# An RWKV-5 and top-1 routing kernel: which engine makes one unit's product of r and k, when the next one's starts, and how many filling products stand between

## The chip, the cores and the metric

The kernel runs on one core of a Trainium2 chip. Its engines work from queues of their own: TensorE (PE, with its weight loads as PEld), VectorE (DVE), ScalarE (ACT), GpSimd (POOL) and SyncE (SP), which issues most DMA transfers. The metric is the device time of one execution in microseconds. Four runs gave 373.76, 372.63, 371.24 and 370.20 us, a median of 371.93 us. The profiled execution is a further one, with a time of its own.

## What is computed

The reference has two parts. The first is a linear attention with decay (RWKV-5), for 4 batches, 8 heads, 768 tokens and a head size of 48:

```python
for t in range(S):
    kt, vt, rt = (k[:, :, t], v[:, :, t], r[:, :, t])
    cur = np.einsum('bhd,bhe->bhde', u[None] * kt, vt)
    y[:, :, t] = np.einsum('bhd,bhde->bhe', rt, state + cur)
    state = w[None, :, :, None] * state + np.einsum('bhd,bhe->bhde', kt, vt)
```

The second takes the 3072 tokens of 384 channels through a top-1 mixture of 8 experts: the expert is the argmax of `x @ w_gate`, and the output is the gate's probability times `relu(x @ w1[e]) @ w2[e]`, with 1024 hidden channels. Everything is FP32.

## The kernel before

The attention is cut into 16 units (`U`), each of one batch and two heads. A unit's 768 tokens are six chunks (`G`) of 128 (`C`). Within a chunk the recurrence becomes matrix products, and between chunks a small state is scanned. Unit `i` takes these steps, which the text calls by the names of the functions:

- `load_rk(i)`, `load_vk(i)`: SP issues the transfers of the unit's r and k (channels on partitions) and of v and k (tokens on partitions). There are three buffers for the first and four for the second, so `load_rk(i + 3)` has to wait for the last reader of unit `i`'s buffer.
- `scale(i)` (L272): VectorE multiplies r and k by powers of the decay, 112 x 1536 elements, into `RK`.
- `pairs(i)` (L278): the product of r and k, 112 x 768 elements, into `rp`, which has two buffers. It reads the loaded r and k, not the scaled ones. POOL makes it unless an engine is given; for unit 0 it is VectorE.
- `keys(i)` (L282): keys times decay, into `Kd`, on POOL unless an engine is given; it needs `T3`, which ScalarE copies once at the start.
- `p_own(i)` (L291): TensorE multiplies `rp` by the bonus u into a part of the bank `dsb`; `own_t(i)` (L295) transposes that on VectorE; `diag(i)` (L309) lets ScalarE write twelve diagonal blocks with it into `A`.
- `p_scores(i)` (L303): the chunks' 128 x 128 scores from `RK`, into the banks `X01` and `X23`; `mask(i, 0..2)` (L315, L317) copies their strict triangles over the diagonal blocks on VectorE.
- `p_ds(i)` (L326) and `scan(i)` (L331): each chunk's state and the scan over chunks.
- `p_out(i)` (L346, L351): the outputs, into the banks `yps`; `out_t(i)` (L356) copies them on ScalarE; `p_tr(i)` (L364) turns them to tokens on partitions and adds the router's logits.

The whole is under `tc.manual_schedule()`: no planner moves anything. Each engine executes its instructions in the order in which the program emits them, and waits only where data or a buffer make it wait. So the order of calls is the order of every queue. Two helpers exist for the order alone. `p_fill(n, o)` (L115) lets TensorE multiply the identity by itself `n` times into a bank; nothing reads the result, and each product stands in the profile as two records. A copy of one element into `turn` on POOL holds POOL's queue until the element copied from is there: at L730 the token is taken from unit 1's scaled r and k, at L760 from unit 2's, and in later passes (L754) from `own`.

The change touches the end of the prologue (L726 to L738), where unit 0 is being finished and unit 1 prepared, and the first pass (`i == 1`) of the loop `for i in range(1, U)`. In that pass come `load_rk(4)`, `p_own(1)`, `own_t(1)`, `p_scores(1)`, `scale(2)`, `pairs(2)`, `load_rk(5)`, `keys(2)`, `diag(1)`, the masks, `p_ds(1)`, `scan(1)`, and `p_out(0)`. The fill of eight products stands behind unit 0's last scores and ahead of `p_own(1)`. Behind the loop the eight experts follow: early passes of 160 tokens for two of them, then late passes for all.

Of the kernel before, what the change touches and what calls it, by code (L numbers as in the profile page):

```python
# [40 lines left out]
def bc(ap, shape):  # L41
    return ap.to_broadcast(shape)


def straight(tc, rk, vk, w, w1, w2, out, flag):
# [8 lines left out]
    nc = tc.nc  # L54
# [10 lines left out]
    yps = [pp.tile([128, 512], FP32, name=f"yps{k}") for k in range(2)]  # L65
# [25 lines left out]
    def load_rk(i):  # L91
        if i < U:
            b, hp = divmod(i, HP)
            if i < 3:
                nc.sync.dma_start(rks[i % 3][0:KP], rk[b, hp].rearrange("h p u s -> (h p) u s")[0:KP])
            else:

                for h in range(2):
                    nc.sync.dma_start(rks[i % 3][64 * h:64 * h + D], rk[b, hp, h, 0:D])

    def load_vk(i):
        if i < U:
            b, hp = divmod(i, HP)
            nc.sync.dma_start(vks[i % 4], vk[b, hp])
# [7 lines left out]
    def p_fill(n, o):  # L112

        for _ in range(n):
            nc.tensor.matmul(o, lhsT=ident, rhs=ident, start=True, stop=True, skip_group_check=True)  # L115
# [50 lines left out]
    def p_key_decay(h0, nh):  # L166
        for hp in range(h0, h0 + nh):
            nc.tensor.transpose(tr[:, hp * 128:hp * 128 + KP], T3c[:, hp, :], ident[0:KP, 0:KP])
        nc.scalar.copy(T3[:, h0:h0 + nh].rearrange("p a (h d) -> p a h d", h=2),
                       tr[:, h0 * 128:(h0 + nh) * 128].rearrange("p (a h d) -> p a h d", a=nh, h=2)[:, :, :, 0:D])  # L170
# [18 lines left out]
    turn = cp.tile([1, 1], FP32, name="turn")  # L189
# [8 lines left out]
    def numbers():  # L198
        nc.gpsimd.tensor_copy(tri, strict)
        nc.gpsimd.memset(ones, 1.0)  # L200
        nc.gpsimd.iota(it[:, 0:E], pattern=[[-1, E]], base=E, channel_multiplier=0)
        nc.gpsimd.tensor_copy(rev, it[:, 0:E])
        nc.gpsimd.iota(it[:, E:2 * E], pattern=[[N // 128, E]], base=0, channel_multiplier=0)
        nc.gpsimd.tensor_copy(osum, it[:, E:2 * E])

    def more_numbers():
        nc.gpsimd.iota(it[:, 24:32], pattern=[[1, E]], base=0, channel_multiplier=0)
        nc.gpsimd.tensor_copy(num, it[:, 24:32])
        nc.gpsimd.iota(it[:, 2 * E:3 * E], pattern=[[N, E]], base=0, channel_multiplier=0)
        nc.gpsimd.tensor_copy(basef, it[:, 2 * E:3 * E])  # L210
        for a in range(4):
            q = slice(32 * a, 32 * a + 32)
            nc.gpsimd.iota(it[q, 32:32 + ng], pattern=[[32, ng]], base=0, channel_multiplier=1)
        nc.gpsimd.tensor_copy(pos, it[:, 32:32 + ng])
        nc.gpsimd.iota(it[:, 48:52], pattern=[[128, 4]], base=0, channel_multiplier=1)
        nc.gpsimd.tensor_copy(pos2, it[:, 48:52])
# [34 lines left out]
    RKs = [ca.tile([128, 2, S], FP32, name=f"RK{i}") for i in range(3)]  # L251
# [18 lines left out]
    def scale(i):  # L270
        hp, x = i % HP, rks[i % 3]
        nc.vector.tensor_tensor(RKs[i % 3][0:KP].rearrange("p u (c t) -> p u c t", t=C),  # L272
                                x[0:KP].rearrange("p u (c t) -> p u c t", t=C),
                                bc(TT[:, hp, :, None, :], [KP, 2, G, C]), op=ALU.mult)

    def pairs(i, eng=None):
        x = rks[i % 3]
        (eng or nc.gpsimd).tensor_tensor(rps[i % 2][0:KP], x[0:KP, 0], x[0:KP, 1], op=ALU.mult)  # L278

    def keys(i, eng=None):  # L280
        hp, v = i % HP, vks[i % 4]
        (eng or nc.gpsimd).tensor_tensor(Kds[i % 2], v[:, G:2 * G - 1, :], bc(T3[:, hp, None, :], [128, G - 1, 2 * D]),  # L282
                                         op=ALU.mult)

    def p_own(i):


        hp = i % HP
        x = rps[i % 2][0:KP].rearrange("p (c a j) -> p a c j", a=4, j=32)
        for a in range(4):  # L290
            nc.tensor.matmul(dsb[32 * a:32 * a + 2, 240:240 + 32 * G].rearrange("p (c j) -> p c j", j=32),  # L291
                             lhsT=ubs[:, hp, :], rhs=x[:, a], start=True, stop=True, skip_group_check=True)

    def own_t(i):
        nc.vector.transpose(own[i % 2].rearrange("p c m -> p (c m)"), dsb[:, 240:240 + 32 * G])  # L295

    def p_scores(i, cs):
        r = RKs[i % 3]
        for c in cs:
            for h in range(2):  # L300
                q = slice(64 * h, 64 * h + D)
                o = X01[h][:, c, :] if c < 4 else X23[:, h, (c - 4) * C:(c - 3) * C]
                nc.tensor.matmul(o, lhsT=r[q, 1, c * C:(c + 1) * C], rhs=r[q, 0, c * C:(c + 1) * C],  # L303
                                 start=True, stop=True, skip_group_check=True)

    def diag(i):
        A = Aw[i % 2]
        for c, h in [(c, 0) for c in range(4)] + [(c, 1) for c in range(4)] + [(c, h) for h in range(2) for c in (4, 5)]:
            nc.scalar.activation(A[:, place(c, h), :], ident, func=ACT.Copy, scale=own[i % 2][:, c, h:h + 1])  # L309

    def mask(i, k):
        A = Aw[i % 2]
        m = strict.bitcast(I32)
        if k < 2:
            nc.vector.copy_predicated(A[:, 4 * k:4 * k + 4, :], bc(m[:, None, :], [128, 4, C]), X01[k])  # L315
        else:
            nc.vector.copy_predicated(A[:, 8:12, :].rearrange("p (h c) t -> p h c t", h=2),  # L317
                                      bc(m[:, None, None, :], [128, 2, 2, C]),
                                      X23[:, :, 0:2 * C].rearrange("p h (c t) -> p h c t", c=2))
# [34 lines left out]
    def out_t(i):  # L354
        for k in range(2):
            nc.scalar.copy(yTs[i % 3][0:KP, k], yps[k][0:KP, 0:S // 2])  # L356
# [71 lines left out]
    def p_count():  # L428
        nc.tensor.matmul(dsb[:, 480:480 + E], lhsT=ones, rhs=osum, start=True, stop=True, skip_group_check=True)

    def count(dst):
        nc.vector.tensor_tensor(dst, dsb[:, 480:480 + E], basef, op=ALU.subtract)
# [293 lines left out]
    diag(0)  # L726
    p_key_decay(1, HP - 1)
    load_rk(3)
    scale(1)
    nc.gpsimd.tensor_copy(turn, RKs[1][0:1, 0, 0:1])  # L730
    pairs(1)
    keys(1)
    p_ds(0)
    scan(0)
# [1 line left out]
    mask(0, 1)  # L736
    p_scores(0, range(4, G))
    mask(0, 2)  # L738
    p_fill(8, yps[0][:, 384:512])
    load_vk(3)  # L740
    for i in range(1, U):
        b, k = divmod(i - 6, 4)
        rt = i >= 6 and k == 0 and b < B - 1
        if i == 1:
            load_rk(4)
        p_own(i)
        if i == 12:
            p_count()
        own_t(i)
        if i == 12:  # L750
            count(cnt2)
            nc.vector.tensor_scalar(out=viol[:, 12:14], in0=cnt2[:, 0:2], scalar1=float(EARLY), scalar2=None, op0=ALU.is_lt)
        if i > 1:
            nc.gpsimd.tensor_copy(turn, own[i % 2][0:1, 0, 0:1])  # L754
        behind = i > 6 and i % 4 == 3
        p_scores(i, range(4 if behind else G))
        if i + 1 < U:
            scale(i + 1)
            if i == 1:
                nc.gpsimd.tensor_copy(turn, RKs[2][0:1, 0, 0:1])  # L760
            pairs(i + 1)
            load_rk(i + 4)
            keys(i + 1, nc.vector if i in (7, 8, 11, 12) else None)
        if i == 3:
            numbers()
        if i == 5:
            more_numbers()
        diag(i)
        mask(i, 0)
        mask(i, 1)  # L770
        if 2 <= i:
            p_tr(i - 2)
        p_ds(i)
        if rt:
            p_rank(b)
            slots(b)
        scan(i)
        if behind:
            p_scores(i, range(4, G))
        if rt:  # L780
            mask(i, 2)
        if 2 <= i:
            keep(i - 2)
        if not rt:
            mask(i, 2)
        if i == U - 1:
            for p in early:
                p.xT()
        if rt:
            gates(b)  # L790
            total(b, nc.gpsimd)
            ids(b)
        if i in sends:
            send(*sends[i])
        p_out(i - 1)
        out_t(i - 1)
        if i % 4 == 1 and i > 4:
            choose((i - 5) // 4)
        load_vk(i + 3)
        if 2 <= i < 6:  # L800
            clear(2 * i - 4)
        if i == 12:
            weights1(0, (0, 1))
        if i == 13:
            for p in early:
                p.load()
        if i == 14:
            weights1(0, (2, 3))
# [666 lines left out]
```

## Time and profile before

| | |
|---|---|
| Median of four runs | 371.93 us (370.20 to 373.76) |
| Profiled execution, its own time | 373.38 us |
| Span of that execution | 371.5 us |
| Mean granted TensorE clock | 0.984 |
| Busy in the span | PE 355.7 us (96%), PEld 336.6, DVE 263.0, ACT 142.9, POOL 204.5 |
| HBM traffic | 52.02 MB read, 11.40 MB written |
| `scale` (L272), VectorE | 16 times, 1723 ns each |
| `pairs` (L278), POOL | 15 times, 1959 ns each on average |
| `pairs` (L278), VectorE | once, at 9.09 us, 954 ns |
| Fill ahead of unit 1 (L115) | 16 records from 14.74 us, 3.63 us |

Times in the profile count from the first instruction of the span. A group's line gives line, engine, operation, the tiles written and read, the shapes and how often. "Idle before" is the time in which the engine had nothing to do ahead of such an instruction, with what ended it. The clock row (PEclk) is the share of full TensorE speed that the chip granted, in tenths for each of 40 slices of 9.3 us; the same figure stands as a number where busy times are given by stretches. The chain that ended last goes back from the last instruction, at each step to what released it.

### The profile page before, as it was taken

Reading aid. Unit: us, or ns where it says so; the run is one execution under the profiler, and the core shown is the slowest. Engines: PE = TensorE matmul, PEld = TensorE weight load, DVE = VectorE, ACT = ScalarE, POOL = GpSimd, SP = SyncE. Lnnn points to the kernel's source line nnn. Section 1 sums busy time; section 2 is a strip of 40 time slices with the busy share of each in tenths; the row PEclk is TensorE's granted clock in tenths of the full one; section 3 lists DMA queues with packets and bytes.
Section 4 is the critical chain, followed back from the end, with each engine's and each line's share of the span. In section 5 each row is a group of like instructions: output and inputs, shape, how many; then the busy total and the mean of one; then the engine's idle time right before and its main releaser. Section 6 shows DMA issues by size and latency. Waiting matters only on the chain.

```text
span 371.5 us, 9106 instructions
## 1 busy us (share of the span) xinstructions
PE 355.7 (96%) x3355; PEld 336.6 (91%) x3355; DVE 263.0 (71%) x653; ACT 142.9 (38%) x411; POOL 204.5 (55%) x242
## 2 busy tenths in 40 slices
PE   5999999999898899999999999999999999999991
PEld 5788888888787899999999999999999999999891
DVE  6797886896873317785697996788788789765531
ACT  2487877876883320232222312221230221113210
POOL 5377888988963350372213605913931950999341
PEclk9699999999999999999999999999999999999997
DMA  7999987888646595777748425733843853313401
GB/s 204 257 213 250 239 215 198 250 217 221 221 101 213 180 360 169 173 211 258 191 142 207 127 69 182 191 112 95 213 147 110 182 167 116 119 50 84 146 18 51
DMA packets 35253, 63.81 MB, mean 172 GB/s; under 512 B 18873, under 2 KB 19913, under 8 KB 35200
## 3 DMA queue, kind: packets, MB, share of 16 engines
q1 hardware_dynamic: 29696, 48.59, 49.7%
q0 software_dynamic: 3776, 9.84, 7.4%
q10 hardware_dynamic: 1728, 4.72, 4.0%
q8 instruction: 28, 0.46, 0.5%
q14 instruction: 25, 0.20, 0.2%
HBM read 52.02 MB, written 11.40 MB: 171 GB/s over the span
## 4 chain that ended last, share of the span: by engine, by line
PE 90%; DVE 3%; DMA 2%; issue 2%; ACT 1%; POOL 1%; POOLq 0%; SPq 0%; DVEq 0%; ACTq 0%
PE X L507 12%; PE X L569 10%; PE yps L611 8%; PE X L485 8%; PE tr L611 8%; PE X L303 7%; PE yps L507 5%; PE yps L346 5%; PE tr L364 4%; PE dsb L611 3%; PE tr L507 3%; PE dsb L507 3%; PE yps L351 3%; PE yps L569 2%; PE dsb L326 2%; PE dsb L291 2%
## 5 line engine op out<-in xcount | busy, mean ns | idle before, releaser
L684 POOL DMA_INDIRECT out_dram<-yo,ix x28 | 28.4, 1014 | 68.1 <-DVE so L629 43.1
L309 ACT ACTIVATE A<-ident,own 128x128 f32<-128x128 f32 x192 | 58.2, 391 | 11.4 <-DVE own L295 9.9
L418 POOL DMA_INDIRECT rows<-xb,slot x24 | 29.7, 1236 | 13.2 <-issue 4.8
L569 PE MATMUL X<-hT,w2s 128*128 128x160 f32 (+5 forms) x288 | 36.5, 287 | 0.0
L569 PEld LDWEIGHTS X<-hT,w2s 128*128 128x128 f32 x288 | 36.2, 191 | 0.2
L611 PE MATMUL yps<-tums,sums 128*128 128x192 f32 x184 | 32.4, 326 | 0.0
L303 PEld LDWEIGHTS X<-RK 48*128 48x128 f32 x384 | 23.6, 191 | 7.5 <-issue 4.6
L611 PEld LDWEIGHTS yps<-tums,sums 128*128 128x128 f32 x184 | 30.3, 190 | 0.0
L303 PE MATMUL X<-RK 48*128 48x128 f32 x384 | 27.9, 288 | 2.3 <-DVE RK L272 2.3
L278 POOL TENSOR_TENSOR rp<-rk 112x768 f32<-112x768 f32 x15 | 29.4, 1959 | 0.0
L272 DVE TENSOR_TENSOR RK<-rk,TT 112x1536 f32<-112x1536 f32 x16 | 27.6, 1723 | 1.7 <-DMA rk<-in_rk_dram 1.7
L684 POOL DMA_INDIRECT out_dram<-yt,it x16 | 16.8, 1048 | 20.5 <-DVE so L629 9.3
L315 DVE COPY_PREDICATED A<-strict,X 128x512 f32<-128x512 int32 x32 | 23.2, 740 | 4.7 <-ACT A L309 4.7
L507 PE MATMUL X<-xT,w1s 128*128 128x208 f32 (+5 forms) x120 | 26.0, 331 | 0.0
L698 POOL TENSOR_TENSOR tums<-w2s,tums 128x384 f32<-128x384 f32 x24 | 24.7, 1028 | 0.4
L346 PE MATMUL yps<-A,vk 128*48 128x128 f32 x384 | 24.0, 274 | 0.0
L507 PEld LDWEIGHTS X<-xT,w1s 128*128 128x128 f32 x120 | 20.9, 190 | 0.0
L346 PEld LDWEIGHTS yps<-A,vk 128*48 128x48 f32 x384 | 20.2, 123 | 0.5
L364 PE MATMUL tr<-sel,yT 112*128 112x104 f32 x128 | 18.5, 287 | 2.1 <-ACT yT L356 1.5
L640 ACT ACTIVATE so<-so,xg 128x192 f32<-128x192 f32 x24 | 10.1, 452 | 25.3 <-DVE so L629 21.9
L364 PEld LDWEIGHTS tr<-sel,yT 112*128 112x128 f32 x128 | 15.6, 191 | 4.5 <-ACT yT L356 1.7
L356 ACT COPY yT<-yps 112x384 f32<-112x384 f32 x32 | 14.0, 482 | 14.9 <-PE yps L351 7.3
(214 smaller groups left out, 826.2 us busy)
## 6 DMA issues: line engine op xcount, KB each, us to landing
w1s<-in_w_dram SPq DMA_DIRECT2D x36, 384.0 KB
w2s<-in_w_dram SPq DMA_DIRECT2D x24, 384.0 KB
vk<-in_vk_dram SPq DMA_DIRECT2D x16, 528.0 KB
rk<-in_rk_dram SPq DMA_DIRECT2D x26, 288.0 KB
w2s<-in_w_dram ACTq DMA_DIRECT2D x8, 384.0 KB
xs<-rows SPq DMA_DIRECT2D x16, 169.0 KB
rk<-in_rk_dram SPq DMA_DIRECT2D x3, 672.0 KB
w1s<-in_w_dram ACTq DMA_DIRECT2D x4, 384.0 KB
```

The lines of the kernel that those rows point to most:

```text
L272: nc.vector.tensor_tensor(RKs[i % 3][0:KP].rearrange("p u (c t) -> p u c t", t=C), x[0:KP].rearrange("p u (c t) -> p u c t", t=C), bc(TT[: ...
L278: (eng or nc.gpsimd).tensor_tensor(rps[i % 2][0:KP], x[0:KP, 0], x[0:KP, 1], op=ALU.mult)
L303: nc.tensor.matmul(o, lhsT=r[q, 1, c * C:(c + 1) * C], rhs=r[q, 0, c * C:(c + 1) * C], start=True, stop=True, skip_group_check=True)
L309: nc.scalar.activation(A[:, place(c, h), :], ident, func=ACT.Copy, scale=own[i % 2][:, c, h:h + 1])
L346: nc.tensor.matmul(o(c, h), lhsT=v[:, c, h * D:(h + 1) * D], rhs=A[:, place(c, h), :], start=c < 2, stop=c == 0, skip_group_check=True)
L364: nc.tensor.matmul(trv[c // 4][:, c % 4, :], lhsT=yTs[i % 3][0:KP, c & 1, (c // 2) * C:(c // 2 + 1) * C], rhs=sel[:, c & 1, i % HP, :], st ...
L418: s_ = nc.gpsimd.indirect_dma_start(out=rows[:, :], out_offset=bass.IndirectOffsetOnAxis(ap=slot[b % 2][:, c:c + 1], axis=0), in_=xbs[b % ...
L485: nc.tensor.matmul(p[:, 0:self.n], lhsT=w1s[self.k % 2][f // 2][:, m, f % 2 * 128:(f % 2 + 1) * 128], rhs=self.t[:, m, 0:self.n], start=m ...
L507: nc.tensor.matmul(p[:, at * n:(at + 1) * n], lhsT=a, rhs=b, start=j == 0, stop=j == len(ab) - 1, skip_group_check=True)
L569: nc.tensor.matmul(p[:, 0:n], lhsT=w2s[self.k % 2][f // 2][:, f % 2, m * 128:(m + 1) * 128], rhs=self.h[:, f, self.c:self.n], start=f == 0 ...
L611: nc.tensor.matmul(p[:, at * Z:(at + 1) * Z], lhsT=a(f), rhs=b(f), start=f == 0, stop=f == FT // 2 - 1, skip_group_check=True)
L684: s_ = nc.gpsimd.indirect_dma_start(out=to[:, :], out_offset=bass.IndirectOffsetOnAxis(ap=at, axis=0), in_=x, in_offset=None, bounds_check ...
```

## The change

It has three parts. The product of unit 1, `pairs(1)`, moves from POOL to VectorE and ahead of `scale(1)` in VectorE's queue; the token at L730 that held POOL until `scale(1)` goes with it. The token at L760 that held POOL until `scale(2)` goes too, so that POOL may begin `pairs(2)` as soon as its data and buffer are there. And of the eight filling products ahead of `p_own(1)` two remain there, while two more are put between `p_own(1)` with its transposition and `p_scores(1)`.

```diff
     diag(0)
     p_key_decay(1, HP - 1)
     load_rk(3)
+    pairs(1, nc.vector)
     scale(1)
-    nc.gpsimd.tensor_copy(turn, RKs[1][0:1, 0, 0:1])
-    pairs(1)
     keys(1)
     p_ds(0)
     scan(0)
@@ -736,7 +735,7 @@
     mask(0, 1)
     p_scores(0, range(4, G))
     mask(0, 2)
-    p_fill(8, yps[0][:, 384:512])
+    p_fill(2, yps[0][:, 384:512])
     load_vk(3)
     for i in range(1, U):
         b, k = divmod(i - 6, 4)
@@ -753,11 +752,11 @@
         if i > 1:
             nc.gpsimd.tensor_copy(turn, own[i % 2][0:1, 0, 0:1])
         behind = i > 6 and i % 4 == 3
+        if i == 1:
+            p_fill(2, yps[0][:, 384:512])
         p_scores(i, range(4 if behind else G))
         if i + 1 < U:
             scale(i + 1)
-            if i == 1:
-                nc.gpsimd.tensor_copy(turn, RKs[2][0:1, 0, 0:1])
             pairs(i + 1)
             load_rk(i + 4)
             keys(i + 1, nc.vector if i in (7, 8, 11, 12) else None)
```

## The prediction

> **What bounds the kernel now.** I read the page first: what limits the span, and whether the TensorE clock was whole.
>
> ```profile
> PEclk9699999999999999999999999999999999999997
> PE 90%; DVE 3%; DMA 2%; issue 2%; ACT 1%; POOL 1%; POOLq 0%; SPq 0%; DVEq 0%; ACTq 0%
> ```
>
> TensorE is 90% of the chain that ended last, and its clock is whole except in the second slice (9.3 to 18.6 us), which is where the change lies. Next come the busy times in stretches of 3.41 us, cut where the clock row changes.
>
> ```profile
> 11.25:14.67 3.42, 3.42 (x39) 2.68 (x35) 3.22 (x4) 3.42 (x13) 0.95 (x2) 0.50 1.02 279
> 14.67:18.08 3.41, 3.41 (x17) 3.34 (x16) 1.62 (x3) 0.44 (x2) 2.16 (x2) 0.50 1.06 250
> 18.08:21.49 3.41, 3.41 (x69) 2.84 (x69) 2.62 (x3) 2.20 (x8) 0.46 (x2) 1.00 1.00 212
> ```
>
> Behind length, PE, PE loads, DVE, ACT and POOL stands the granted clock: 0.50 for two stretches, whole from 18.08. The second is filled by the eight products `p_fill(8)`; the first, with PE as busy by the row, did not bring the clock back. The chain in order of time shows the same place.
>
> ```profile
> 13.66 1.16 PE X L303 x8
> 14.81 3.56 PE yps L115 x16
> 18.37 0.48 PE dsb L291 x8
> 18.85 0.02 issue
> 18.87 0.40 DVE own L295
> 19.27 0.02 issue
> 19.29 2.47 ACT A L309 x8
> ...
> 22.55 0.54 DVE S L331
> 23.09 0.14 issue
> 23.22 0.51 PE dsb L291 x8
> 23.73 1.54 PE X L303 x24
> ```
>
> The fill is 3.56 us of the path, though `p_own(1)` (L291 at 18.37) needs only unit 1's product, which POOL ended at 13.86 + 1.81 = 15.67. Then TensorE leads to the end of the loop. Last, the waits of 12 to 24 us.
>
> ```profile
> POOL turn L760 <- DVE RK L272: 4.2, 1, 4.2
> DVE own L295 <- PE dsb L291: 2.6, 1, 2.6
> PEld dsb L291 <- POOL rp L278: 0.3, 1, 0.3
> ```
>
> VectorE idles 2.6 us behind the fill, POOL 4.2 us for unit 2's scaling, and TensorE then 0.3 us for that late product.
>
> **The change, part by part.**
>
> *Fills, eight to four.* A product is two records. In the fill they start 0.372 us (the first) and 0.213 us apart at half clock. Two products: 0.372 + 3 x 0.213 = 1.01 us. So the first pair runs 14.74 to 15.75. `p_own(1)` takes 0.44 us at full clock (18.30 to 18.74); at half clock it costs at least that and at most 0.88. I take 0.65, between[...]: 16.40. The second pair: 17.41. `p_scores(1)` needs 1.54 us at full clock; until 18.08 it has 0.67 us at half clock, worth 0.34, and 1.20 remain: it ends at 19.28 against 18.74 + 1.54 = 20.28. Gain 1.0 us (0.9 to 1.1 with the two ends for `p_own`).
>
> *Unit 1's product on VectorE, ahead of `scale(1)`.* 0.95 us (the one such row, unit 0's at 9.09) against 1.81 on POOL. It starts at 11.99 and ends at 12.94; `scale(1)` then runs to about 14.65 instead of 13.65, and the scan and the three masks of unit 0 behind it are 0.9 us later: the masks end near 15.9, 16.55 and 17.2 instead of 16.28 for the last. Those waiting: `p_scores(1)` overwrites the banks that the masks read, but comes at 17.41; `own_t(1)` is queued behind the masks and runs at 17.2 instead of 18.87. So it costs nothing, under cover of fills and `p_own(1)`, 0.2 us to spare; without that cover, up to 0.9.
>
> *The POOL token ahead of unit 1's product goes, and that product too.* `keys(1)` starts when ScalarE has copied T3 (14.73 + 0.38 = 15.11) instead of 15.63, and ends at 16.3. SP's `load_rk(4)`, which waits for product and scaling of unit 1, is issued at 14.65 instead of 15.69; `load_rk(5)` near 20 instead of 23.0. The DMA share is 1.0 in these stretches, so they land in turn and about when they did: nothing gained.
>
> *Unit 2's product without its token.* It can start when `rk` of unit 2 is there (the trace's completions: 16.36) and runs 16.4 to 18.2 instead of 21.17 to 22.99. `p_own(2)` stops waiting for it: 0.1 us on the path (23.09 to 23.22), the rest of the 0.3 being the load ahead. But now POOL precedes VectorE's `scale(2)`. Two rows of the late stage show what that means:
>
> ```profile
> 205.23 2.82 DVE L698 TENSOR_TENSOR sums<-hT 128x512 f32<-128x512 f32 x1
> ```
>
> This takes 0.68 us in its median; here POOL products ran back to back from 203.62 to 207.5. And POOL's own, behind VectorE:
>
> ```profile
> 90.52 3.90 POOL L278 TENSOR_TENSOR rp<-rk 112x768 f32<-112x768 f32 x1
> ```
>
> 1.82 us elsewhere; it waited out two VectorE products. The Trainium skill's page "SBUF — State Buffer", section "Who interferes with whom", says why: a VectorE instruction with both inputs in SBUF and a GpSimd one that reads SBUF exclude each other, and the first keeps the port to its end. This speaks against the change. Without exclusion `scale(2)` starts at 17.6 (after `own_t(1)`), with it at 18.2; I take 18.2, ending at 19.9 against 20.90. Behind it are unit 1's masks and scan: 20.6, 21.35, 22.0, 22.7, all 1.0 earlier than before. `p_scores(2)`, at 23.66 - 1.1 = 22.6, finds its banks free at 21.35 and, for the part it reaches at 23.6, 22.7. So no loss. If `keys(2)` followed at once (its `vk` lands at 18.68, just behind), `scale(2)` would wait until 19.4, end 0.2 later than before, and leave about 0.5 of the gain.
>
> Sum: 1.0 + 0.1 = 1.1 us off the profiled execution's 373.4 (span 371.5 and 1.9 around it): 372.3. The loop behind is led by TensorE at 6.2 us a unit, and scalings and keys keep over 1.2 us to their transfers (unit 3's `rk` lands at 21.53, its scaling would start near 23), so the shift should reach the end. Against the median 371.93: 370.8.
>
> **What the fills may really be for.** The sum lets the clock come back at 18.08 as before. The skill's "TensorE: Matmul & The Clock Gate", Part 1, says that the half-rate clock is given up after a busy window of about 3.4 us, and that the windows run free of the kernel's start. The changes, at 4.43, 11.25 and 18.08, agree (6.83 us apart, two windows). The rule taken by the busy row would have released the clock at 14.67 (3.42 of 3.42 busy); the trace did not. Part 4 says transposes don't count alike; that window holds 0.82 us of them, and the changed one holds none, so by this it passes. If instead only full products count, the changed window has 2.0 us of fills for 3.3, and fails. The start of the kernel lies between: there fills in 2.98 us of 3.41 sufficed, 2.82 without the 0.16 us by which the first record of a group is longer (0.372 for 0.213); the changed window has 3.34 less four such starts, 2.7; the failed one, by the same count and without transposes, 2.1. Nearer to passing.
>
> **Rivals.**
> 1. *The clock stays at half.* Place: the edge at 18.08, and each behind it. A missed window costs half its length, 1.7 us of TensorE work, since TensorE leads. One miss: -1.1 + 1.7 = +0.6, 372.5. Two: +2.3, 374.2. From three it is slower by over 1% (+4.0, 375.9); four give 377.6. For it: the failed window held just what the loop is made of, 48-row and 48-column products. Against: the loop has no transposes. The upper bound, half clock from 18 to the loop's end at 116, would be +98 us; I take three to four windows, as the rows show no more than one in a row failing.
> 2. *The gain is eaten.* Where the free windows fall so that the clock is whole at 14.7, fills were cheap before (0.112 us a record: 0.9 saved), and `p_scores(1)` then waits for the later masks: its start goes from about 16.2 to 16.6, +0.4. With `scale(2)` behind POOL, which without fills would start near 16.8 instead of 18.2, up to +0.7: 372.3 to 372.6. The four runs' spread of 3.6 us suggests that such executions exist.
> 3. *The product's early start does nothing*, because the path is the fill alone: 0.1 less, 370.9, not to be told from the forecast.
> 4. *More than expected*: besides the shift one half-rate window fewer: -2.8, 369.1; to pass 1% takes yet another.
>
> **How the numbers follow.** Forecast (with 3) 0.42: 370.8, within 369.0 to 372.5. Gain eaten 0.12. One or two missed windows 0.09. Three or more 0.32, half of it below 378. More than 1% faster 0.05. 1% is 3.7 us, about what a measurement of this kernel can tell from no change. So faster 0.05, same 0.42 + 0.12 + 0.09 = 0.63, slower 0.32. The range 369.0 to 378.0 leaves out 0.05 below and 0.15 above; the likeliest sign's own is 369.0 to 372.5.
>
> **What would show it.** Right: fill records 8 instead of 16; `p_own(1)` near 15.8, `p_scores(1)` near 17.4, `p_ds(1)` near 19.3 (20.27 before); POOL's product of unit 2 near 16.4; `scale(2)` starting only as it ends, at 18.2; no wait of `p_own(2)` for POOL; the clock whole by 18.1 or wherever that execution's edge lies, and each unit about 1.1 us earlier. Wrong: a clock row of 5s and 6s in the slices past 18 us; `p_scores(1)` waiting for a mask; `scale(2)` running past 20.9.

## The result and the profile after

The changed kernel is slower: its time is 1.0039 times that of the kernel before, with a 95% interval of 1.0025 to 1.0052. The medians are 372.45 us (52 runs) and 371.01 us (78 runs), so about 1.4 us are lost where 1.1 us were to be won. That lies inside the stated range, but on the other side of no change.

The profiled execution of the changed kernel took 371.05 us, with a span of 369.1 us. That is less than the 371.5 us of the one shown of before, although the kernel is slower. Its clock row says why the two can't be set side by side (the clock in 40 slices, and the head of the chain that ended last):

```profile
PEclk9999999999999999999999999999999999999997
PE 90%; DVE 4%; DMA 2%; issue 1%; ACT 1%; POOL 0%; POOLq 0%; SPq 0%; DVEq 0%
```

This execution had the whole clock up to TensorE's last work; the one of before had 6.8 us at half clock ahead of it. Each run is listed with its mean granted clock, and the profiles show what this mean stands for: 0.993 to 0.997 where the clock did not fall ahead of TensorE's last work, 0.988 or 0.991 with 3.4 us at half ahead of it, 0.981 to 0.987 with 6.8 or 10.2 us. So the runs can be sorted at 0.990, which leaves at most one stretch of 3.4 us at half in a run above it. Of the changed kernel's 54 listed executions 28 are of the first kind, with a median of 371.02 us, and 26 of the second, with 373.16 us. The kernel before, in the 93 runs listed beside the experiments, was of the second kind in only 17. So the execution that the prediction worked from (0.984) was of the rarer kind.

What leads the changed kernel is seen in its chain in order of time, from 12 to 24 us:

```profile
11.79 0.78 DVE rp L278
12.58 0.00 issue
12.58 0.95 DVE RK L272
13.53 0.72 issue
14.25 0.65 DVE S L331
14.89 1.25 DVE A L315 x2
16.14 0.62 DVE A L317
16.77 0.27 DVE own L295
17.03 0.02 issue
17.06 2.47 ACT A L309 x8
19.53 1.23 DVE A L315 x2
20.76 0.64 DVE S L331
21.41 0.14 issue
21.54 0.51 PE dsb L291 x8
```

Where the fill stood on the path before, VectorE's queue stands now, from unit 1's product to the scan of unit 1, with unit 1's diagonal blocks on ScalarE between. TensorE leads only from `p_own(2)` at 21.54 on. The waits of 9 to 24 us give the price:

```profile
PE dsb L291 <- DVE S L331: 2.2, 2, 1.2
```

Twice `p_own` waited for a scan, for 1.2 us and 1.0. And the rows in order of time show what made the second scan late:

```profile
16.16 1.81 POOL L278 TENSOR_TENSOR rp<-rk 112x768 f32<-112x768 f32 x1
...
16.94 2.65 DVE L272 TENSOR_TENSOR RK<-rk,TT 112x1536 f32<-112x1536 f32 x1
```

`scale(2)` stands with 2.65 us instead of 1.72: POOL's product, now ahead of it, ended at 17.97, and 17.97 + 1.72 = 19.69 is about where the scaling ended (19.59). The chain names ScalarE's eighth diagonal block, ended at 19.53, ahead of the two masks. But the first mask needs only the first four; it stood behind the scaling in VectorE's queue, so scaling and eighth block were equally late.

### The profile page after: what moved, and what is told of

The parts are those of the page before. It is cut to its first block, busy times and chain, and to the rows that moved or that the text cites. A ratio compares the mean times of both kernels' runs of the same rounds, so it can differ in the third digit from the quotient of the medians.

```text
span 369.1 us, 9084 instructions
## 1 busy us (share of the span) xinstructions
PE 352.8 (96%) x3347; PEld 333.8 (90%) x3347; DVE 264.5 (72%) x654; ACT 142.7 (39%) x411; POOL 203.4 (55%) x239
## 4 chain that ended last, share of the span: by engine, by line
PE 90%; DVE 4%; DMA 2%; issue 1%; ACT 1%; POOL 0%; POOLq 0%; SPq 0%; DVEq 0%
PE X L507 12%; PE X L569 10%; PE X L485 9%; PE yps L611 8%; PE tr L611 8%; PE X L303 6%; PE yps L507 5%; PE yps L346 5%; PE tr L364 4%; PE dsb L611 4%; PE tr L507 3%; PE dsb L507 3%; PE yps L351 3%; PE yps L569 2%; PE dsb L326 2%; PE X L364 2%
## 5 line engine op out<-in xcount | busy, mean ns | idle before, releaser
L272 DVE TENSOR_TENSOR RK<-rk,TT 112x1536 f32<-112x1536 f32 x16 | 28.5, 1781 | 1.5 <-DMA rk<-in_rk_dram 1.5
L684 POOL DMA_INDIRECT out_dram<-yt,it x16 | 16.8, 1048 | 20.5 <-DVE so L629 9.3
L278 POOL TENSOR_TENSOR rp<-rk 112x768 f32<-112x768 f32 x14 | 27.5, 1965 | 0.0
L645 ACT COPY so<-tr 128x192 f32<-128x192 f32 x7 | 2.2, 321 | 44.5 <-PE tr L611 44.5
```

What stands on the lines that cost most here:

```text
L684: s_ = nc.gpsimd.indirect_dma_start(out=to[:, :], out_offset=bass.IndirectOffsetOnAxis(ap=at, axis=0), in_=x, in_offset=None, bounds_check ...
```

## The experiments

Two theories were set against each other. One (P) says that the loss lies in the order of VectorE and POOL: POOL's early product holds up `scale(2)`, and `p_own(2)` waits for the scan behind it. The other (first C, then F) says that the loss comes from the four missing fills, by way of the clock. Runs of one group shared a chip and its runs of the kernel before; chips differ by some 5 us, so only times of one group are compared directly.

### A longer fill at the start, to keep the clock whole

Four kernels had more filling products at the very start. The first is the kernel before with this edit:

```diff
-    p_fill(17, X01[1][:, 0, :])
+    p_fill(26, X01[1][:, 0, :])
```

> The kernel before, with 26 instead of 17 filling products at the very start, so that TensorE no longer rests from 6.9 to 9.2 us. Both theories: the clock stays whole from its first release on (granted mean 0.993 or more in every run), and the time is that of the fastest runs of the kernel before, about 369.3 us against a median of 371.0.

Measured: 1.0023 times before (1.0002 to 1.0043), 371.01 us. All 12 runs had a granted mean of 0.993 or more, as expected; but only 2 of the 23 runs of the kernel before on this chip were under 0.990, so 12 runs do not show that the edit did it. The gain was not there, and TensorE's rows show a cost:

```profile
4.59 5.44 PE L115 MATMUL X<-ident 128*128 128x128 f32 x38
9.96 0.72 PE L303 MATMUL X<-RK 48*128 48x128 f32 x8
```

The fill, slow until the clock's first release (at 6.75 us in this execution), ran until 10.03 us, and the first scores came at 9.96 instead of 9.23 us. The edit costs at least what it saves.

The changed kernel with the same edit:

> The changed kernel with the same 26 products. Theory P (VectorE's chain: unit 1's product delays scan 0, for which p_own(1) waits, and POOL's early product holds up scale(2), so that scan 1 and with it p_own(2) come late): still slower than long_before by about 1.5 us, 370.8, with scale(2) at 2.65 us and p_own(2) waiting about 1.0 us for scan 1. Theory C (the change only loses by the clock's gate, as fewer fills keep it at half for longer): with the clock whole the loss is gone, 369.3 or up to 0.4 less.

Measured: 1.0089 (1.0052 to 1.0127), 374.15 us, and 0.0066 more than the kernel above. The longer fill at the start did not keep its clock whole: 4 of 7 runs were under 0.990. In the profile `scale(2)` was held up for longer than either theory had it:

```profile
17.13 1.82 POOL L278 TENSOR_TENSOR rp<-rk 112x768 f32<-112x768 f32 x1
...
17.86 3.87 DVE L272 TENSOR_TENSOR RK<-rk,TT 112x1536 f32<-112x1536 f32 x1
...
18.91 1.21 POOL L282 TENSOR_TENSOR Kd<-vk,T 128x480 f32<-128x480 f32 x1
```

Here (rows in order of time) `keys(2)` followed the product without a gap, and the scaling had to wait for both: 20.12 + 1.72 = 21.84, recorded end 21.73. TensorE then rested 2.20 us ahead of `p_own(2)`, and the clock fell to half at 24.64.

The same with POOL's token for unit 2 back:

```diff
             scale(i + 1)
+            if i == 1:
+                nc.gpsimd.tensor_copy(turn, RKs[2][0:1, 0, 0:1])
             pairs(i + 1)
```

> As long_after, but the token that holds POOL's product of unit 2 behind scale(2) is back. Theory P: scale(2) takes 1.72 us again instead of 2.65, scan 1 ends 0.9 us earlier, p_own(2) then waits for POOL's product instead, and the time is 0.5 to 0.9 us under long_after, 369.9 to 370.3. Theory C: as long_after.

Measured: 1.0081 (1.0049 to 1.0114), 373.0 us; `scale(2)` was back at 1.72 us and `p_own(2)` at 20.84, as theory P has it, but the time fell by less than the two intervals can tell apart, and 4 of 7 runs were again under 0.990. In the profiled one of them the clock fell only at 135.06 us, behind a rest of 2.94 us in which TensorE waited for ScalarE in an expert's early pass. A low mean alone does not tell where the clock fell, and this did not settle the matter.

And the kernel before with the longer start and without the eight products:

```diff
-    p_fill(8, yps[0][:, 384:512])
```

> As long_before, without the eight products ahead of p_own(1). Theory P: with the clock whole these products end at about 15.7 us, just when POOL's product of unit 1 is there, so taking them away changes less than 0.2 us: 369.2 to 369.4. Theory C: without them TensorE rests for 1.8 us, the clock falls to half in some runs, and the time rises to 370 or more.

Measured: 1.0067 (1.0039 to 1.0095), 372.47 us. Theory P missed here, and C was right: TensorE rested 2.37 us ahead of `p_own(1)`, the clock fell to half at 16.14, and 6 of 10 runs were under 0.990. So the eight products are of use: they hold the clock while VectorE and POOL prepare unit 1.

### Each part of the change alone

On one chip, whose kernel before had a median of 365.54 us. First the whole change with only the token put back:

> The changed kernel with only the token put back that holds POOL's product of unit 2 behind scale(2). Known by now: in runs with a whole clock (granted mean 0.990 or more) the kernel before has a median of 369.6 us, the changed one 371.0; and the changed one has a stretch at half clock in half of its runs. Theory P (POOL's early product, and with it keys(2), holds up scale(2), so p_own(2) waits for scan 1): scale(2) is back at 1.72 us, p_own(2) comes near 20.6 instead of 21.5, and the runs with a whole clock fall by about 0.9 to 370.1. Theory F (it is only the missing four fills): no change, 371.0.

Measured: 1.0015 (0.9990 to 1.0040), 366.62 us. `scale(2)` took 1.72 us again. `p_own(2)` came at 22.36 in the profile, later than theory P has it, as that execution had half clock from 17.01 to 20.43; of its 12 runs 9 were at 0.990 or more, with a median of 366.00 against 365.39 for such runs of the kernel before. By the median most of the loss was gone, with the four fills still missing, though the interval reaches into that of the changed kernel.

The kernel before with only that token taken away:

```diff
-            if i == 1:
-                nc.gpsimd.tensor_copy(turn, RKs[2][0:1, 0, 0:1])
             pairs(i + 1)
```

> The kernel before with only the token for unit 2's product taken away; eight fills and everything else as before. Theory P: POOL ends keys(1) at about 16.8 us and starts the product just ahead of scale(2), which then takes 2.6 to 3.9 us; with a whole clock 1 to 2 us slower than before, 370.6 to 371.6. Theory F: no change, or a little faster as the product is there earlier: 369.4 to 369.6.

Measured: 1.0057 (1.0024 to 1.0091), 368.58 us. This one deletion costs about as much as the whole change. The row of the scaling, and then the stretches behind it, cut where the clock changed:

```profile
16.29 3.62 DVE L272 TENSOR_TENSOR RK<-rk,TT 112x1536 f32<-112x1536 f32 x1
```

```profile
16.60:20.01 3.41, 3.41 (x80) 3.06 (x76) 3.41 (x2) 3.41 (x12) 3.23 (x2) 1.00 1.00 205
20.02:23.43 3.41, 1.75 (x32) 1.29 (x30) 3.32 (x6) 1.40 (x5) 1.46 (x2) 1.00 1.03 235
```

```profile
23.43:26.80 3.37, 3.37 (x22) 3.10 (x18) 2.40 (x3) 3.37 (x12) 3.37 (x3) 0.50 1.03 220
26.85:30.25 3.40, 3.40 (x45) 3.14 (x44) 1.27 (x2) 0.39 (x2) 0.86 (x2) 0.50 1.03 234
```

The scaling waited here for two POOL instructions without a gap between them, `keys(1)` (15.33 to 16.53) and the product (16.50 to 18.30): 18.30 + 1.72 = 20.02, recorded end 19.91. In the stretches TensorE, its loads, VectorE, ScalarE, POOL and the clock come behind the length. TensorE is busy 1.75 of 3.41 us while `p_own(2)` waits 1.7 us for the late scan; the next two stretches have half clock. That is the second half of the price: 9 of 12 runs were under 0.990, against 7 of 35 of the kernel before. Theory P had foreseen the held scaling but not what the clock adds. It had 1 to 2 us for the runs with a whole clock; the three at 0.990 or more have a median of 365.80 against 365.39, so on this chip nearly the whole loss lies in the runs with the lower clock.

The kernel before with only the fills changed (two, and two behind `p_own(1)`):

> The kernel before with only the fills changed, eight to two and two. Theory F: the clock falls to half in about half of the runs instead of one in ten, and the runs with a whole clock come near 371.0. Theory P: as p_own(1) waits for POOL's product until 15.7 either way, the fills cost nothing with a whole clock but for the two behind it (0.45 us): 369.6 to 370.1; half-clock stretches come oftener, since TensorE rests for about 1.7 us.

Measured: 1.0055 (1.0030 to 1.0079), 368.25 us; no run was above 0.991, and 7 of 12 were under 0.990. Here F was right, and P too low. In the profile the fewer fills show in how long the clock stayed low. It fell at 11.38, ahead of the changed fills, behind a rest of TensorE from 6.97 to 9.17, much as in the kernel before. There the stretch with the eight products, 14.67 to 18.08, was busy throughout and the clock came back behind it. Here the same stretch held a rest of 0.21 us, in which `p_own(1)` waited for POOL's product, and the clock came back one stretch later. That the rest decided it is not shown, as the clock stayed at half behind a wholly busy stretch too (23.43 to 26.80 above):

```profile
7.97:11.38 3.41, 1.96 (x25) 1.26 (x25) 3.11 (x5) 0.38 (x2) 0.00 (x0) 1.00 1.02 242
11.38:14.79 3.41, 3.41 (x37) 2.60 (x35) 3.22 (x4) 3.41 (x13) 0.85 (x2) 0.50 1.04 269
14.79:18.21 3.42, 3.21 (x18) 2.04 (x20) 2.88 (x5) 1.20 (x5) 2.25 (x2) 0.50 1.05 223
18.21:21.62 3.41, 3.41 (x46) 3.19 (x46) 2.00 (x3) 2.65 (x10) 2.64 (x3) 0.50 0.99 221
```

The kernel before with only unit 1's product moved:

```diff
+    pairs(1, nc.vector)
     scale(1)
-    nc.gpsimd.tensor_copy(turn, RKs[1][0:1, 0, 0:1])
-    pairs(1)
```

> The kernel before with only unit 1's product moved to VectorE ahead of scale(1). Both theories put this part near nothing: p_own(1) comes some 0.5 us earlier behind the fills, but scan 0 and the three masks 0.9 us later, so own_t(1) and scale(2) start within 0.3 us of before: 369.3 to 370.0 with a whole clock. If instead the wait of p_own(1) for scan 0 is the main loss, it is slower by 0.7 or more.

Measured: 1.0001 (0.9980 to 1.0021), 365.81 us; 11 of 12 runs at 0.990 or more. This part costs nothing, as forecast.

### The fills against the token, with unit 1's product on VectorE

Another chip, with 369.47 us for the kernel before. The changed kernel once more:

> The changed kernel itself, to stand beside the next ones on one chip. 0.4% slower than the kernel before: with a whole clock (granted mean 0.990 or more) about 1.4 us slower, and a stretch at half clock in about half of its runs.

Measured: 1.0051 (1.0018 to 1.0084), 371.53 us; 6 of 12 runs under 0.990. At 0.990 or more its median is 370.93 against 369.31, so 1.6 us are lost without the longer stretches at half clock. `scale(2)` took 2.91 us, `p_own(2)` came at 22.0.

With the eight fills back, and the token still gone:

```diff
-    p_fill(2, yps[0][:, 384:512])
+    p_fill(8, yps[0][:, 384:512])
...
-        if i == 1:
-            p_fill(2, yps[0][:, 384:512])
```

> The changed kernel with the eight fills back ahead of p_own(1) and none behind it; unit 1's product stays on VectorE, unit 2's without its token. Theory P (POOL ahead of scale(2) is the main loss): scale(2) is still held up, 2.6 us or more, p_own(2) still waits for scan 1, and the time stays 0.2 to 0.4% over the kernel before, though TensorE rests less and the clock falls in fewer runs. Theory F (the four missing fills are the loss): as the kernel before, within 0.1%.

Measured: 1.0054 (1.0022 to 1.0086), 371.69 us: no better than the changed kernel. Theory F fails. This kernel and the one with only unit 1's product moved differ in nothing but the token, and their intervals, each against the kernel before on its own chip, don't overlap, if only just (1.0022 and 1.0021). VectorE's scaling and masks and TensorE's `p_own(2)`, first without the token and then with it:

```profile
17.07 2.97 DVE L272 TENSOR_TENSOR RK<-rk,TT 112x1536 f32<-112x1536 f32 x1
...
19.97 1.34 DVE L315 COPY_PREDICATED A<-strict,X 128x512 f32<-128x512 int32 x2
...
21.99 0.51 PE L291 MATMUL dsb<-rp,wug 112*2 112x192 f32 x8 [1.34 <-DVE S L331]
```

```profile
16.65 1.72 DVE L272 TENSOR_TENSOR RK<-rk,TT 112x1536 f32<-112x1536 f32 x1
...
19.25 0.75 DVE L315 COPY_PREDICATED A<-strict,X 128x512 f32<-128x512 int32 x1 [0.21 <-ACT A L309]
...
20.68 0.51 PE L291 MATMUL dsb<-rp,wug 112*2 112x192 f32 x8 [0.43 <-DVE S L331]
```

`p_own(2)` is where TensorE takes the lead. It comes 1.3 us later here, but 0.4 of that stood ahead of the scaling already. Counted from `own_t(1)` (16.78 and 16.36), the scaling takes 1.25 us more and `p_own(2)` comes 0.89 later. The other profiles in which VectorE leads agree: `p_own(2)` comes 4.3 us behind `own_t(1)` where the scaling takes 1.72 us, 4.9 where it takes 2.65 or 2.68, 5.2 with 2.91 or 2.97, 5.85 with 3.62 and 6.08 with 3.87. So all but 0.36 us of the hold is passed on. That part is hidden because without the hold the second mask waits for ScalarE's eighth block, as the row at 19.25 shows.

Then the token not at the product but behind it, at `keys(2)`:

```diff
             pairs(i + 1)
             load_rk(i + 4)
+            if i == 1:
+                nc.gpsimd.tensor_copy(turn, RKs[2][0:1, 0, 0:1])
             keys(i + 1, nc.vector if i in (7, 8, 11, 12) else None)
```

> The changed kernel with a token that holds keys(2), not the product of unit 2, behind scale(2). Theory P, with POOL's instructions taking the port one behind another: scale(2) takes 2.7 us at most, as only the product can precede it, against up to 3.9; p_own(2) never waits more than about 1.2 us. The time lies between the changed kernel and the one with the token at the product: 0.2 to 0.35% over the kernel before. If keys(2) played no part, it equals the changed kernel.

Measured: 1.0038 (1.0010 to 1.0067), 371.06 us, with 2.68 us for `scale(2)`. Its longest run, 372.91 us, is shorter than the changed kernel's 374.23, but the intervals overlap: what `keys(2)` adds to the changed kernel is not settled by these runs.

Last, a try for a version that beats both:

```diff
-    p_fill(17, X01[1][:, 0, :])
+    p_fill(21, X01[1][:, 0, :])
...
+    pairs(1, nc.vector)
     scale(1)
-    nc.gpsimd.tensor_copy(turn, RKs[1][0:1, 0, 0:1])
-    pairs(1)
```

> A try for a version that beats both: the kernel before with unit 1's product on VectorE (alone that was even), and 21 instead of 17 filling products at the very start. If the pause of TensorE around 7 to 9 us is what brings the half clock, this has none, without the 0.7 to 0.9 us that 26 products put ahead of the first scores when the clock is late: 0.1 to 0.3% faster than the kernel before. If the first scores come late all the same: up to 0.2% slower.

Measured: 1.0020 (0.9984 to 1.0056), 370.0 us; 4 of 12 runs under 0.990. No gain. No kernel of this study beats the one before. This one has unit 1's product on VectorE and the token, on the chip of the last three; at 0.990 or more its median is 369.75, against 370.56 to 370.93 for those without the token at the product. These 0.8 to 1.2 us are about what `p_own(2)` shows; the 0.4 us between 369.75 and the 369.31 of the kernel before are left open.

### What holds the scaling

These are the changed kernel with the token back, and other POOL work in the place that the early product had. Each ran once (374.78, 372.27 and 368.24 us; the kernel before once on each chip, 371.11, 371.11 and 364.70), so only the profiles are read.

```diff
+        if i == 1:
+            for _ in range(4):
+                x = vks[1].rearrange("p a b -> p (a b)")[:, 0:nz]
+                nc.gpsimd.tensor_tensor(zt, x, x, op=ALU.mult)
```

> The changed kernel with the token back at unit 2's product, and in its place on POOL four products of other data (unit 1's v by itself, into a scratch tile), about 0.8 us each and back to back from about 16.3 to 19.5 us. Port theory: scale(2), wanted at about 17, is held until they end and takes 3.5 us or more, though it shares no data with them. Data theory (it is the common r and k): 1.72 us.

Measured: a miss for the port theory's number. `scale(2)` took 1.72 us, as it came first in the small gap behind the first of the four products, all writing one tile. It was POOL that waited: the four products took 4.64 us together, one of them 2.29 us instead of 0.70. So the two exclude each other on unrelated data, but not in the order foreseen.

```diff
+        if i == 1:
+            for _ in range(8):
+                nc.gpsimd.memset(zt, 0.0)
```

> The same with eight POOL fills of the scratch tile with zeros, which only write, 0.35 us each from about 16.3 to 19.1 us. Port theory, by the reading port: scale(2) takes its 1.72 us beside them. If any POOL work holds it: 2.8 us or more.

Measured: POOL's fills and the scaling side by side, both at their usual lengths (0.36 us each fill; rows of POOL and of VectorE):

```profile
16.05 3.27 POOL L757 MEMSET zt<- 128x312 f32 x8
...
17.02 1.72 DVE L272 TENSOR_TENSOR RK<-rk,TT 112x1536 f32<-112x1536 f32 x1
```

And one product that is surely under way:

```diff
+        if i == 1:
+            x = vks[1].rearrange("p a b -> p (a b)")
+            nc.gpsimd.tensor_tensor(xbs[2].rearrange("p a b c -> p (a b c)")[:, 0:1056], x, x, op=ALU.mult)
```

> As pool_reads, but a single POOL product of unit 1's v and k by themselves, 128 x 1056 elements into an unused tile, from about 16.1 to 18.6 us (1056 elements at the 2.4 ns each of POOL's 112 x 768 product), on data that scale(2) does not touch. Port theory: scale(2), wanted at 16.7 to 17.1, is recorded at 3.2 to 3.7 us, that is it ends 1.7 us behind POOL's product. Data theory: 1.72 us.

Measured:

```profile
16.00 1.94 POOL L757 TENSOR_TENSOR xb<-vk 128x1056 f32<-128x1056 f32 x1
...
17.01 2.55 DVE L272 TENSOR_TENSOR RK<-rk,TT 112x1536 f32<-112x1536 f32 x1
```

POOL's product was shorter than estimated, so the number was missed (2.55 for 3.2), but the rule held: the scaling ended 1.62 us behind the end of a product with which it shares no data (16.00 + 1.94 = 17.94, and 19.56). POOL reading SBUF holds it; POOL only writing does not. This is what the Trainium skill states in "SBUF — State Buffer", section "Who interferes with whom"; the runs agree with it.

## Why the prediction was wrong

*The bound.* The reading of the profiled execution was right for that execution: the fill was on the path, and TensorE led behind it. The mistake was to take it for the kernel. It had 6.8 us at half clock, and a mean as low as that is found in about one run in five of the kernel before; with it, the fill ends at 18.30, and everything on VectorE and POOL has 2.6 us to spare. With a whole clock the fill ends before POOL's product of unit 1 is there (with only the token of unit 2 away the fill ended at 14.94, and `p_own(1)` waited for POOL until 15.41), and nothing of that spare time is left. The row of the clock and the runs' spread both hinted at it, and the prediction put the case down as a rival.

*Fills.* Gain of 1.0 us: not there in the ordinary case. In the profile of after, `p_own(1)` came at 14.95 and then `p_scores(1)` at 16.03, both early, but they lead to nothing, as `p_own(2)` waits for the scan. With the token's effect away, four fills fewer show no gain either (1.0015), and alone they lose half a percent, with no run above 0.991. Why they cost so much less beside unit 1's early product is not shown. The prediction's point on what the fills are for was right.

*Unit 1's product.* Costed at nothing under cover of fills and `p_own(1)`: right in the sum (1.0001 alone, with the eight fills). One wait had been missed: `p_own(1)` waits for scan 0 (1.2 us of rest in the profile of after), as both use the bank `dsb`.

*Unit 2's product without its token.* This is the step that failed. "So no loss" rested on `scale(2)` standing at 19.18 in the profile of before, so that 18.2 was still early. With a whole clock it is wanted at 16.7 to 17.1, and the hold, rightly foreseen down to the rule, makes it 0.9 to 1.3 us longer in the four profiles without the token there, which is a loss and not a shorter gain. Masks and scan pass on all but 0.36 us of it to `p_own(2)`. Rival 2 had this mechanism with about the right start times (16.8 and 18.2), and its 0.7 us lies within the 0.6 to 0.9 us by which `p_own(2)` is late. It left out the clock, and got a chance of 0.12.

*Who waits for whom.* The 0.1 us that `p_own(2)` was to win were read from a wait row that names POOL's product. The chain shown beside it had the scan of unit 1 directly ahead of `p_own(2)` (22.55, then 23.22): both were nearly equally late. Taking the product earlier could win nothing while the scan stayed, and the step made the scan later.

*Rival 1, the clock staying at half.* It had 0.32 for three missed windows or more and over 1% lost; that did not come. But the clock is the other part of the loss: 26 of 54 executions of the changed kernel are under 0.990, at 2.1 us more than the others. No trace of the changed kernel holds one of these lower clocks. In kernels close to it the clock fell anew where TensorE waits for the two scans: at 17.01 behind scan 0 (changed, with the token back), at 23.43 and 24.64 behind scan 1 (only the token away; long start, changed). A missed window was seen too, behind both of the last two: 3.41 us of loop work without a rest, and the clock came back one window later. The fear that the loop's own products can't bring the clock back is refuted: in the rows of the kernel with only its fills changed, 18.21 to 21.62 holds loop work alone, and the clock is whole behind it.

*The number.* 370.8 us was forecast from a base of 371.93, the median of four runs; with 78 it is 371.01. Corrected for that the forecast was 369.9 against 372.45.

## What to carry to other kernels

A change is costed for the clock that most runs have: where the clock row of the profiled execution shows a fall, ask what the path looks like without it before any slack in that stretch is spent. Work that one engine can do early is not free when it shares a port with the engine that leads: a copy of one element that holds it back can be worth half a percent. And before a wait is removed, look in the chain for the next release of the same instruction.

## What was not expected of the hardware

- VectorE's waiting instruction is not served between POOL instructions that follow each other without a gap: the scaling took 3.87 us behind two of them (17.13 to 20.12), though the second began while it waited. With a gap of 0.08 us (16.63 to 16.71, in the run with four products) VectorE came first.
- How little rest lowers the clock. In all 17 profiles each change of the clock lies a whole multiple of 3.41 us behind its first release (before: 4.43, 11.25, 18.08; only the token away: 6.36, 23.43, 30.25). So the edges of such windows can be counted on where nothing changed. By TensorE's busy row:

| Window | Kernel | TensorE busy, us | Clock behind it |
|---|---|---|---|
| 12.73 to 16.14 | long start, no eight fills | 1.04 | half |
| 21.23 to 24.64 | long start, changed | 1.21 | half |
| 20.02 to 23.43 | only the token away | 1.75 | half |
| 7.84 to 11.25 | before | 1.77 | half |
| 5.62 to 9.04 | changed | 1.86 | whole |
| 7.97 to 11.38 | only fills | 1.96 | half |
| 13.60 to 17.01 | changed, token back | 2.06 | half |
| 18.77 to 22.18 | changed, eight fills | 2.07 | whole |
| 13.48 to 16.89 | POOL writes | 2.10 | half |
| 12.45 to 15.86 | changed | 2.25 | whole |
| 19.27 to 22.69 | changed | 2.40 | whole |

  Over all windows up to 355 us that began with a whole clock, in all profiles, up to 1.77 us of work were always followed by half clock, 2.11 and more never, and between them (1.86 to 2.10) both are found. So a rest of 1.3 us within a window, far shorter than the window, can lower the clock, and one of 1.64 us or more did so each time; what decides between them is not shown. As the edges fall differently in each execution, the same rest can lie in one window or be split over two.
